# One rotation of six single PSUM banks in place of two mixing banks and two gram pairs

## The chip, the cores and the metric

The kernel runs on one core of a Trainium2 chip. The metric is device time in microseconds (us): the median of three runs. Beside it stands one profiled execution, whose trace gives start and length of each instruction; all times below that are not called a median are places or lengths in that execution, counted from the start of its span.

## The reference

An RWKV-6 attention block is followed by an MLP mixer. Batch 4, 8 heads, 768 steps, head width 48, all in fp32:

```python
for t in range(S):
    cur = einsum('bhd,bhe->bhde', u * k_t, v_t)
    y[:, :, t] = einsum('bhd,bhde->bhe', r_t, state + cur)
    state = w_t[..., None] * state + einsum('bhd,bhe->bhde', k_t, v_t)
x = y.transpose(0, 2, 1, 3).reshape(B, S, H * D)           # 4 x 768 x 384
h = relu(x^T @ w_tok1) @ w_tok2                             # over the 768 tokens, 256 hidden
u = x + h^T
out = u + relu(u @ w_ch1) @ w_ch2                           # over the 384 channels, 1536 hidden
```

## The kernel before

**Attention** is computed in chunks of 64 steps. A unit is 256 steps of one batch with all heads, so there are three units a batch and twelve in all. For each unit VectorE scans the decays twice (`ends` L354 and `begins` L362, over 112 x 1041 elements) and scales keys (L359) and queries (L365) by them. TensorE turns the keys (`tokens`, L276, copied out by ScalarE at L277), multiplies keys and queries of each chunk (`gram`, L248), makes the outer products of keys and values (`carry`, `kv_ps` L293), and then the outputs: the part from earlier chunks (`before`, `y_ps` L306) and that from within the chunk (`after`, L320). The gram is masked by VectorE into `at` (`mask`, L403). For the first four units there is a second gram with the bonus u (`own_gram`), put on the diagonal by a predicated copy (`own_put`, L376); later units get the diagonal from VectorE sums instead (L391). The states are passed from chunk to chunk by ScalarE (`scaled`, L416) and VectorE (`update`, L426, which reads `kv_ps`).

**Mixing** of a batch has these steps: `hidden` (L494) and `back` (L501, added to x by VectorE at L503) over tokens; `turn`, which transposes x (L510, copied out by ScalarE at L511); then for each 256 tokens `up` (twelve tiles `z_ps`, L518, taken by ScalarE with a relu at L520) and `down`. The first `down` is plain (L589, `h_ps`); all others are `quarters`: seven products `q_ps` of six matmuls each (L607) in Strassen's manner, from sums that VectorE makes of z (L648 to L650). The products are taken one by one: the first by ScalarE (L616), the next by VectorE at L621, L625, L629, L633, L639 and L645. The last batch uses `thirds` (L550) in place of `up`.

**Order.** The mixing of batch n is woven with the attention of batch n+1: `woven` merges the two lists by their shares of cost, and `strict` fixes the resulting order on TensorE, VectorE and ScalarE. So each of these engines runs a fixed list, in order. The attention of the first batch stands alone in front, with an order written out by hand; the last batch's mixing stands alone at the end.

**PSUM** has eight banks of 128 x 2 KiB. Until the last batch they belong to three pools: `ps_m`, two single banks that serve all mixing tiles (`h_ps`, `z_ps`, `q_ps`) and, in the first batch, the turned keys; `ps_g`, two pairs of banks for grams, turned keys and the transposes of x; and `ps_a`, one pair for `kv_ps` and `y_ps`. A tile may be written as soon as the readers of the tile that had its bank before are done. For the last batch, `ps_g` and `ps_a` are closed and six single banks (`ps_c`) take their place for `thirds` and the transposes, beside the two of `ps_m`.

A branch for rare inputs at the end (`by_halves`) is built from the same functions and is not executed here.

Of the kernel before, what the change touches and what calls it, by code (L numbers as in the profile page):

```python
# [10 lines left out]
f32 = mybir.dt.float32  # L11
# [9 lines left out]
DM = H * D  # L21
T = 64
C = S // 128
UC = 2
UB = C // UC
NU = B * UB
A = H // 2
# [3 lines left out]
X = UC * A  # L31
# [31 lines left out]
def rwkv6_then_mixer(  # L63
# [18 lines left out]
    pe, dve, act, pool, sp = nc.tensor, nc.vector, nc.scalar, nc.gpsimd, nc.sync  # L82
# [20 lines left out]
    xpool = ctx.enter_context(tc.tile_pool(name="xpool", bufs=2))  # L103
    wide = ctx.enter_context(tc.tile_pool(name="wide", bufs=1))
    mpool = ctx.enter_context(tc.tile_pool(name="mpool", bufs=2))
    ps_m = ctx.enter_context(tc.tile_pool(name="ps_m", bufs=2, space=bass.MemoryType.PSUM))
    six_banks = ctx.enter_context(ExitStack())

    def for_attention():
        return [six_banks.enter_context(tc.tile_pool(name=name, bufs=n, space=bass.MemoryType.PSUM)) for name, n in (("ps_g", 2), ("ps_a", 1))]  # L110

    ps_g, ps_a = for_attention()

    rks = [const.tile([128, 2 * COLS], f32, name=f"rk{i}") for i in range(3)]
    ws = [const.tile([128, WCOLS], f32, name=f"w{i}") for i in range(2)]
# [10 lines left out]
    strictly = const.tile([128, T], f32, name="strictly")  # L126
    diagonal = const.tile([128, T], u8, name="diagonal")
# [115 lines left out]

    def grams(k_, r_):

        g = ps_g.tile([128, 2, 512], f32, name="gram")
        for ca in range(X):
            fours(lambda q, j, rows, cols: pe.matmul(  # L248
                g[cols, q, ts(ca, T)], k_[rows, ds(ca * 128 + j * T, T)], r_[rows, ds(ca * 128 + j * T, T)],
                start=True, stop=True))  # L250
        return g.rearrange("p q (x t) -> p q x t", x=X)

    def over_heads(mask):
        return mask.unsqueeze(1).unsqueeze(1).to_broadcast([128, 2, X, T])

    def by_u(k_, uk, a):
        of, to = (t.rearrange("p (c a n) -> p c a n", c=UC, a=A)[:ROWS, :, a, :] for t in (k_, uk))
# [2 lines left out]
    def all_by_u(k_):  # L260
        uk = apool.tile([128, COLS], f32, name="near", bufs=1)
        for a in range(A):
            by_u(k_, uk, a)
        return uk

    def turned_keys(k_, apart=False):

        kT = apool.tile([128, UC, A, 128], f32, name="kT", bufs=1)
        if apart:
            both = [ps_m.tile([128, 512], f32, name="k_ps", tag="m").rearrange("p (a t) -> p a t", a=A) for c in range(UC)]  # L270
        else:
            both = ps_g.tile([128, 2, 512], f32, name="gram").rearrange("p c (a t) -> p c a t", a=A)
            both = [both[:, c] for c in range(UC)]
        for c in range(UC):
            for a in range(A):
                pe.transpose(both[c][:, a, :], k_[:, ts(c * A + a, 128)], ident)  # L276
        return kT, [lambda c=c: act.copy(kT[:, c], both[c]) for c in range(UC)]  # L277
# [50 lines left out]
    def unit(i):  # L328

        bt, half = divmod(i, UB)  # L330
        r_, k_ = (rks[i % 3][:, ts(n, COLS)] for n in range(2))
        w_, at = ws[i % 2], ats[i % 2]
        by_chunk = [t[:ROWS].rearrange("p (g t) -> p g t", t=T) for t in (r_, k_)]
        L = {"before": {}}
# [38 lines left out]
            L["own"] = grams(L.pop("uk"), r_)  # L373

        def own_put():
            dve.copy_predicated(out=at, mask=over_heads(diagonal), data=L.pop("own"))  # L376

        def products(n):
            t = nears[i]
# [11 lines left out]
            dve.copy_predicated(out=at, mask=over_heads(diagonal), data=of.unsqueeze(3).to_broadcast([128, 2, X, T]))  # L391

        def tokens():
            L["kT"], L["copies"] = turned_keys(k_, apart=bt == 0)

        def copied(c):
            L["copies"][c]()
# [2 lines left out]
            L["gram"] = grams(k_, r_)  # L400

        def mask():
            dve.tensor_mul(at, L.pop("gram"), over_heads(strictly))  # L403

        def carry():
            L["kv"] = outer(L.pop("kT"), vs[i], half, (ps_g, "gram") if i == UB - 1 else (ps_a, "a"))
# [78 lines left out]
    def mixing(bt, x_of, out_rows):  # L485
        last = bt == B - 1
# [17 lines left out]

        def turn(c):

            ps = bank("xT_ps") if last else ps_g.tile([128, 2, 512], f32, name="xT_ps", tag="gram")[:, 0]
            ps = ps[:, :DM].rearrange("p (m t) -> p m t", t=128)
            for m in range(DM // 128):
                pe.transpose(ps[:, m, :], x_of()[:, c, ts(m, 128)], ident)  # L510
            act.copy(xT[:, :, ts(c, 128)], ps)  # L511
# [155 lines left out]
    def steps(i):  # L667
# [38 lines left out]
           *e2["taken"], lambda: (load_w(3), load_rk(3), load_v(UB), load_w(4), load_rk(4)), to_ch[0][0], to_ch[1][0],  # L706
           *e1["ranges"], *h[8:], *e2["ranges"], lambda: sp.dma_start(u_rows, u_all))

    def single(steps, n):
        return [(0.1, f) for f in steps[n < 2:]]  # L710

# [2 lines left out]
    def verdict():  # L714
# [4 lines left out]
        dve.tensor_reduce(out=of_all[0:1], in_=total, axis=mybir.AxisListType.X, op=ALU.add)  # L719
        dve.tensor_scalar(beyond[0:1], of_all[0:1], 0.0, 1.0, op0=ALU.is_le, op1=ALU.is_lt)  # L720
        flagged.append(beyond)

    def bank(name):
        return ps_c.tile([128, 512], f32, name=name, tag="c")

    def last_mixing():
        hiddens, turned, rights, thirds, quarters = mixing_of(B - 1)
# [16 lines left out]
    for bt in range(B):  # L744
        ahead = []
        if bt == 0:
            to_ch = [single(e, n) for n, e in enumerate(to_ch)]
            both = [f for e in zip(ups[0], ups[1]) for f in e]
            ahead = woven(turned, sum(to_ch[:2], []))
            of_weights = [(0.1, lambda n=n: weight_sums(n)) for n in range(4)]  # L750
            pieces = woven(both, sum(to_ch[2:8], [])) + woven(downs[0][:6], to_ch[8]) + woven(downs[0][6:], of_weights[:3])
            pieces += downs[1][:4] + of_weights[3:] + downs[1][4:] + ups[2] + downs[2]
        elif bt < B - 1:
            hiddens, turned, ups, downs = mixing_of(bt)
            pieces = [e for h in hiddens for e in h] + turned
            *pieces, last = pieces
            ups[0].insert(2, last)
            for s in range(S // SEG):
                pieces += ups[s] + downs[s]
        else:  # L760
            six_banks.close()
            ps_c = six_banks.enter_context(tc.tile_pool(name="ps_c", bufs=6, space=bass.MemoryType.PSUM))
            pieces = last_mixing()
        n = (bt + 1) * UB
        att = [e for i in range(n, n + UB) if i < NU for e in steps(i)]
        strict(*(f for _, f in ahead + (woven(att, pieces) if att else pieces)))

    rare = nc.values_load(flagged[0][0:1, 0:1], min_val=0, max_val=1, skip_runtime_bounds_check_because="a comparison's result")

    six_banks.close()  # L770
    ps_g, ps_a = for_attention()

    def by_halves(b):

# [17 lines left out]
        for half in range(UB):  # L792
            r_, k_ = (rks[0][:, ts(n, COLS)] for n in range(2))
            w_, at = ws[0], ats[0]
            sp.dma_start(r_, rk[ds(b * UB + half, 1), 0].rearrange("o p n -> p (o n)"))
            sp.dma_start(k_, rk[ds(b * UB + half, 1), 1].rearrange("o p n -> p (o n)"))
            sp.dma_start(w_, w[ds(b * UB + half, 1)].rearrange("o p n -> p (o n)"))
            vt = vpool.tile([128, UC, DM], f32, name="vt")
            for c in range(UC):
                sp.dma_start(vt[:, c], v[ds(b, 1), ts(half * UC + c, 128), :].rearrange("o p e -> p (o e)"))  # L800
            dve.memset(at, 0.0)
            dve.copy_predicated(out=at, mask=over_heads(diagonal), data=grams(all_by_u(k_), r_))
            decay = rks[1][:, :COLS]
            act.copy(decay[:ROWS].rearrange("p (g t) -> p g t", t=T),
                     w_[:ROWS, :G * SEG1].rearrange("p (g s) -> p g s", s=SEG1)[:, :, 1:])
            for l in range(LEVELS):
                n = 1 << l
                dve.copy_predicated(out=at, mask=over_heads(level_masks[l]), data=grams(k_, r_))
                pair = decay[:ROWS].rearrange("p (m two) -> p m two", two=2)
                rr, kk = (t[:ROWS].rearrange("p (m two n) -> p m two n", two=2, n=n) for t in (r_, k_))  # L810
                for t, mine, other in ((rr, 1, 0), (kk, 0, 1)):
                    dve.tensor_mul(t[:, :, mine], t[:, :, mine], pair[:, :, other].unsqueeze(2).to_broadcast([ROWS, COLS // (2 * n), n]))
                longer = rks[1 + (l + 1) % 2][:, :COLS >> (l + 1)]
                dve.tensor_mul(longer[:ROWS], pair[:, :, 0], pair[:, :, 1])
                decay = longer
            by = decay[:ROWS].rearrange("p (x j) -> p x j", j=2)
            kv = outer(all_turned(k_), vt, half)
            for c in range(UC):
                for j in range(2):
                    g = 2 * (half * UC + c) + j  # L820
                    if g < 2 * C - 1:
                        new = states[g + 1] = apool.tile([128, A, D], f32, name="before", bufs=5)
                        got = kv[:ROWS, j, ds(c * A * D, A * D)].rearrange("p (a e) -> p a e", a=A)
                        if g == 0:
                            dve.tensor_copy(new[:ROWS], got)
                        else:
                            dve.tensor_mul(new[:ROWS], states[g][:ROWS], by[:, ts(c, A), j].unsqueeze(2).to_broadcast([ROWS, A, D]))
                            dve.tensor_add(new[:ROWS], new[:ROWS], got)
            y = across(r_, states, half)
            within(y, at, vt)  # L830
            for f in put_in(x, y, half):
                f()
# [42 lines left out]
```

## Time and profile before

| what | us |
|---|---|
| median of the runs (548.43 to 549.2) | 548.63 |
| the profiled execution | 550.15 |
| its span | 548.4 |
| TensorE busy (matmuls) | 507.8 |
| VectorE busy | 335.8 |
| ScalarE busy | 212.7 |

In the profile PE is TensorE's matmul side and PEld its weight loads, DVE is VectorE, ACT is ScalarE, SP is SyncE, which issues nearly all transfers. `L607` is line 607 of the kernel before. A row of the timeline gives the start, the length, the engine, line and operation, what it writes and reads, how many instructions it merges, and, in brackets, the idle time before it with what ended it. A matrix multiplication of fp32 stands as two instructions, so a product of six is x12. `x12` rows may be short of a record or two. In the list of waits, the numbers are the total, how often, and the longest. The first 60 us are mostly loads and the first batch's attention; after that, busy time of TensorE is given for stretches in the prediction.

### The profile page before, as it was taken

What the parts mean: (1) busy time and instruction counts of PE and PEld (TensorE: products, weight loads), DVE (VectorE), ACT (ScalarE), POOL (GpSimd) and SP (SyncE); (2) the same over time, 40 slices, a digit from 0 to 9 for tenths busy, and PEclk for the clock granted to TensorE, in tenths of its full rate; (3) what the DMA queues carried; (4) which work ended last, traced back from release to release, by engine and by line L of the source; (5) the groups of instructions that cost most, each with busy time, mean ns of one, the idle gap of its engine ahead of it and who ended that gap; (6) DMA issues with size and microseconds to landing.
All of it is one profiled execution on the core that took longest, in us unless ns stands there. A gap on an engine that the chain in (4) does not pass through costs nothing.

```text
span 548.4 us, 12596 instructions
## 1 busy us (share of the span) xinstructions
PE 507.8 (93%) x5542; PEld 435.3 (79%) x5542; DVE 335.8 (61%) x504; ACT 212.7 (39%) x525; POOL 1.3 (0%) x10
## 2 busy tenths in 40 slices
PE   3569899899799999999899999999999999999995
PEld 3556578666698868888888967888888968999995
DVE  7997599878772754192380665295393525775653
ACT  3676776662233333423323324413414313431300
POOL 0000000000000000000000000000000000000000
PEclk9678999899999999999999999999999999999999
DMA  8956656622231403203123113002000000000000
GB/s 304 330 165 209 182 178 241 172 89 84 87 108 34 139 17 117 59 32 125 46 78 92 45 44 99 30 1 88 1 30 1 2 29 2 1 1 31 0 31 33
DMA packets 20941, 46.01 MB, mean 84 GB/s; under 512 B 2128, under 2 KB 13008, under 8 KB 20880
## 3 DMA queue, kind: packets, MB, share of 16 engines
q1 hardware_dynamic: 20736, 45.14, 25.4%
q8 instruction: 45, 0.74, 0.6%
q14 instruction: 16, 0.13, 0.1%
q10 hardware_dynamic: 144, 0.00, 0.0%
HBM read 40.41 MB, written 4.72 MB: 82 GB/s over the span
## 4 chain that ended last, share of the span: by engine, by line
PE 72%; DVE 17%; ACT 6%; DMA 3%; issue 2%; SPq 0%; DVEq 0%; ACTq 0%
PE q_ps L607 21%; PE z_ps L518 21%; PE z_ps L550 6%; PE h_ps L494 5%; PE h_ps L501 4%; PE h_ps L589 3%; PE y_ps L306 3%; DVE to_end L354 3%; PE y_ps L320 2%; PE gram L248 2%; DMA rk<-in_rk_dram 2%; PE kv_ps L293 2%; PE gram L276 1%; DVE z L649 1%; ACT before L416 1%
## 5 line engine op out<-in xcount | busy, mean ns | idle before, releaser
L518 PE MATMUL z_ps<-xT,wch 128*128 128x256 f32 x648 | 149.1, 385 | 1.1 <-DVE o L645 1.1
L518 PEld LDWEIGHTS z_ps<-xT,wch 128*128 128x128 f32 x648 | 120.8, 191 | 18.9 <-DVE o L645 1.9
L607 PE MATMUL q_ps<-wch,z 128*128 128x192 f32 x492 | 87.4, 329 | 0.7 <-DVE o L629 0.5
L607 PEld LDWEIGHTS q_ps<-wch,z 128*128 128x128 f32 x492 | 80.3, 190 | 2.6 <-DVE o L629 1.1
L520 ACT ACTIVATE z<-z_ps 128x256 f32<-128x256 f32 x108 | 41.3, 382 | 84.8 <-PE z_ps L518 84.2
L607 PE MATMUL q_ps<-scratch,z 128*128 128x192 f32 x324 | 57.1, 328 | 3.5 <-DVE o L625 2.9
L607 PEld LDWEIGHTS q_ps<-scratch,z 128*128 128x128 f32 x324 | 52.9, 190 | 4.8 <-DVE o L625 3.8
L416 ACT ACTIVATE before<-state,to_end 112x48 f32<-112x48 f32 x176 | 44.2, 324 | 30.6 <-DVE state L426 28.0
L426 DVE TENSOR_TENSOR state<-before,kv_ps 112x192 f32<-112x192 f32 x40 | 14.0, 350 | 45.1 <-ACT before L416 29.0
L494 PE MATMUL h_ps<-x,wtok 128*128 128x384 f32 x96 | 33.9, 506 | 2.4 <-ACT x L326 2.0
L501 PE MATMUL h_ps<-h,wtok 128*128 128x384 f32 x96 | 35.4, 493 | 0.1
L503 DVE TENSOR_TENSOR x<-x,h_ps 128x384 f32<-128x384 f32 x24 | 13.3, 553 | 33.6 <-PE h_ps L501 33.4
L617 DVE TENSOR_TENSOR o<-x,z 128x192 f32<-128x192 f32 x8 | 2.9, 358 | 49.8 <-ACT z L616 46.7
L494 PEld LDWEIGHTS h_ps<-x,wtok 128*128 128x128 f32 x96 | 18.3, 195 | 14.6 <-ACT x L326 2.8
L354 DVE TENSOR_TENSOR_SCAN to_end<-w,starts 112x1041 f32<-112x1041 f32 (+1 forms) x13 | 28.1, 2160 | 2.0 <-DMA w<-in_w_dram 1.6
L362 DVE TENSOR_TENSOR_SCAN w<-w,starts 112x1041 f32<-112x1041 f32 x12 | 27.9, 2321 | 0.1
L346 ACT ACTIVATE junk<-to_end,least 112x1041 uint8<-112x1041 f32 x12 | 13.9, 1162 | 28.3 <-DVE to_end L354 28.3
L501 PEld LDWEIGHTS h_ps<-h,wtok 128*128 128x128 f32 x96 | 16.6, 190 | 9.6 <-ACT h L496 2.5
L326 ACT COPY x<-y_ps 64x384 f32<-64x384 f32 (+1 forms) x36 | 17.1, 475 | 18.3 <-PE y_ps L320 18.0
L306 PEld LDWEIGHTS y_ps<-before,rk 48*64 48x64 f32 x704 | 14.0, 144 | 12.3 <-issue 10.2
L306 PE MATMUL y_ps<-before,rk 48*64 48x48 f32 x704 | 15.4, 230 | 8.0 <-DVE state L426 8.0
L511 ACT COPY xT<-xT_ps 128x384 f32<-128x384 f32 x24 | 11.4, 476 | 22.0 <-PE xT_ps L510 22.0
(139 smaller groups left out, 668.3 us busy)
## 6 DMA issues: line engine op xcount, KB each, us to landing
rk<-in_rk_dram SPq DMA_DIRECT2D x36, 192.0 KB, 3.7
near<-in_near_dram SPq DMA_DIRECT2D x8, 768.0 KB, 4.5
w<-in_w_dram SPq DMA_DIRECT2D x11, 520.5 KB, 3.4
spare<-in_w_ch_dram SPq DMA_DIRECT2D x10, 512.0 KB, 4.8
vt<-in_v_dram SPq DMA_DIRECT2D x12, 384.0 KB, 3.8
out_dram<-o SPq DMA_DIRECT2D x24, 192.0 KB, 1.9
scratch<-in_w_ch_dram SPq DMA_DIRECT2D x8, 512.0 KB, 4.4
rk<-in_rk_dram SPq DMA_DIRECT2D x6, 512.0 KB, 8.4
```

Of the source, the lines that this page charges most:

```text
L306: pe.matmul(y[put(q, j), q, ds((c * A + a) * D, D)], r_[q * P:q * P + D, ds((c * A + a) * 128 + j * T, T)], before[g][q * P:q * P + D, a, ...
L326: return [lambda: act.copy(x[:, 0], got[:, 0])] + [lambda n=n: act.copy(x[ts(n, P), 1], got[ts(1 - n, P), 1]) for n in range(2)]
L354: dve.tensor_tensor_scan(to, of, start, 0.0, op0=ALU.mult, op1=ALU.add)
L362: dve.tensor_tensor_scan(w_[:ROWS], w_[:ROWS], starts[:ROWS], 0.0, op0=ALU.mult, op1=ALU.add)
L416: act.mul(t[:ROWS, a], state[bt, g][:ROWS, a], by_last(c, j)[:, a:a + 1])
L494: pe.matmul(sums[i], wtok1[:, c, ts(i, 128)], x_of()[:, c, :], start=(c == 0), stop=(c == C - 1))
L501: pe.matmul(ps, wtok2[:, i, ts(c, 128)], h1[:, i, :], start=(i == 0), stop=(i == DTOK // 128 - 1))
L518: pe.matmul(ps, wch1[:, m, ts(jt, 128)], xT[:, m, ts(s, SEG)], start=(m == 0), stop=(m == DM // 128 - 1))
L520: act.activation(zs[s][:, jt, :], ps, AF.Relu)
L550: pe.matmul(ps[:, q], lefts[r][:, ts(q, 128)], of[r], start=first and q == 0, stop=end and q == JB - 1, skip_group_check=True)
L589: pe.matmul(ps, zs[0][:, jt, ts(n, 128)], wch2[:, jt, :], start=(jt == 0), stop=(jt == NJ - 1))
L607: pe.matmul(ps, a[:, j, :], b[:, j, :], start=(j == 0), stop=(j == HJ - 1))
```

## The change

After the first batch's hand-ordered attention (which includes its token-mixing `hidden` step), `ps_g` and `ps_m` are closed, and one pool `ps_m` of six single banks takes their place until the end; `ps_a` keeps its pair throughout. So:

- mixing tiles (`h_ps`, `z_ps`, `q_ps`, and the last batch's `thirds`), grams, turned keys and the transposes of x all come from the six;
- a gram takes two single tiles instead of one pair. Its mask (L403 before) and the diagonal copy (L376 before) then become two instructions of 128 x 512 each instead of one of 128 x 1024;
- the turned keys always use two single tiles;
- in the last batch there are six banks for what had eight.

The function `bank` moves to the top, and nothing else of the order of work is touched. Lines move by up to three: L607 becomes L609, L518 becomes L520, L403 becomes L406, L426 becomes L429.

```diff
-    ps_m = ctx.enter_context(tc.tile_pool(name="ps_m", bufs=2, space=bass.MemoryType.PSUM))
+    ps_a = ctx.enter_context(tc.tile_pool(name="ps_a", bufs=1, space=bass.MemoryType.PSUM))
     six_banks = ctx.enter_context(ExitStack())
-
-    def for_attention():
-        return [six_banks.enter_context(tc.tile_pool(name=name, bufs=n, space=bass.MemoryType.PSUM)) for name, n in (("ps_g", 2), ("ps_a", 1))]
-
-    ps_g, ps_a = for_attention()
+    ps_g, ps_m = (six_banks.enter_context(tc.tile_pool(name=name, bufs=2, space=bass.MemoryType.PSUM)) for name in ("ps_g", "ps_m"))
+
+    def bank(name):
+        return ps_m.tile([128, 512], f32, name=name, tag="m")
...
     def grams(k_, r_):
 
-        g = ps_g.tile([128, 2, 512], f32, name="gram")
+        both = ps_g and ps_g.tile([128, 2, 512], f32, name="gram")
+        g = [both[:, q] for q in range(2)] if ps_g else [bank("gram") for q in range(2)]
         for ca in range(X):
             fours(lambda q, j, rows, cols: pe.matmul(
-                g[cols, q, ts(ca, T)], k_[rows, ds(ca * 128 + j * T, T)], r_[rows, ds(ca * 128 + j * T, T)],
+                g[q][cols, ts(ca, T)], k_[rows, ds(ca * 128 + j * T, T)], r_[rows, ds(ca * 128 + j * T, T)],
                 start=True, stop=True))
-        return g.rearrange("p q (x t) -> p q x t", x=X)
+        if ps_g:
+            return [(slice(0, 2), both.rearrange("p q (x t) -> p q x t", x=X))]
+        return [(slice(q, q + 1), g[q].rearrange("p (q x t) -> p q x t", q=1, x=X)) for q in range(2)]
+
+    def pick(at, mask, of):
+        for q, g in of:
+            dve.copy_predicated(out=at[:, q], mask=over_heads(mask, g.shape[1]), data=g)
...
-    def turned_keys(k_, apart=False):
+    def turned_keys(k_):
...
+        both = [bank("k_ps").rearrange("p (a t) -> p a t", a=A) for c in range(UC)]
...
         def mask():
-            dve.tensor_mul(at, L.pop("gram"), over_heads(strictly))
+            for q, g in L.pop("gram"):
+                dve.tensor_mul(at[:, q], g, over_heads(strictly, g.shape[1]))
...
-            ps = bank("xT_ps") if last else ps_g.tile([128, 2, 512], f32, name="xT_ps", tag="gram")[:, 0]
-            ps = ps[:, :DM].rearrange("p (m t) -> p m t", t=128)
+            ps = bank("xT_ps")[:, :DM].rearrange("p (m t) -> p m t", t=128)
...
+    six_banks.close()
+    ps_g, ps_m = None, six_banks.enter_context(tc.tile_pool(name="ps_m", bufs=6, space=bass.MemoryType.PSUM))
+
...
         else:
-            six_banks.close()
-            ps_c = six_banks.enter_context(tc.tile_pool(name="ps_c", bufs=6, space=bass.MemoryType.PSUM))
             pieces = last_mixing()
```

More of the change, by code (lines that the diff above doesn't have):

```diff
@@ L244, in grams, with over_heads @@
     def grams(k_, r_):
-        g = ps_g.tile([128, 2, 512], f32, name="gram")
+        both = ps_g and ps_g.tile([128, 2, 512], f32, name="gram")
+        g = [both[:, q] for q in range(2)] if ps_g else [bank("gram") for q in range(2)]
         for ca in range(X):
             fours(lambda q, j, rows, cols: pe.matmul(
-                g[cols, q, ts(ca, T)], k_[rows, ds(ca * 128 + j * T, T)], r_[rows, ds(ca * 128 + j * T, T)],
+                g[q][cols, ts(ca, T)], k_[rows, ds(ca * 128 + j * T, T)], r_[rows, ds(ca * 128 + j * T, T)],
                 start=True, stop=True))
-        return g.rearrange("p q (x t) -> p q x t", x=X)
-    def over_heads(mask):
-        return mask.unsqueeze(1).unsqueeze(1).to_broadcast([128, 2, X, T])
+        if ps_g:
+            return [(slice(0, 2), both.rearrange("p q (x t) -> p q x t", x=X))]
+        return [(slice(q, q + 1), g[q].rearrange("p (q x t) -> p q x t", q=1, x=X)) for q in range(2)]
+    def over_heads(mask, n=2):
+        return mask.unsqueeze(1).unsqueeze(1).to_broadcast([128, n, X, T])
+    def pick(at, mask, of):
+        for q, g in of:
+            dve.copy_predicated(out=at[:, q], mask=over_heads(mask, g.shape[1]), data=g)
     def by_u(k_, uk, a):
@@ L264, in all_by_u @@
         return uk
-    def turned_keys(k_, apart=False):
+    def turned_keys(k_):
         kT = apool.tile([128, UC, A, 128], f32, name="kT", bufs=1)
[L269 to L273, printed above, removed]
+        both = [bank("k_ps").rearrange("p (a t) -> p a t", a=A) for c in range(UC)]
         for c in range(UC):
@@ L375, in own_put @@
         def own_put():
-            dve.copy_predicated(out=at, mask=over_heads(diagonal), data=L.pop("own"))
+            pick(at, diagonal, L.pop("own"))
         def products(n):
@@ L393, in tokens @@
         def tokens():
-            L["kT"], L["copies"] = turned_keys(k_, apart=bt == 0)
+            L["kT"], L["copies"] = turned_keys(k_)
         def copied(c):
@@ L721, in verdict @@
         flagged.append(beyond)
-    def bank(name):
-        return ps_c.tile([128, 512], f32, name=name, tag="c")
     def last_mixing():
@@ L768, in rwkv6_then_mixer @@
     rare = nc.values_load(flagged[0][0:1, 0:1], min_val=0, max_val=1, skip_runtime_bounds_check_because="a comparison's result")
-    six_banks.close()
-    ps_g, ps_a = for_attention()
     def by_halves(b):
@@ L801, in by_halves @@
             dve.memset(at, 0.0)
-            dve.copy_predicated(out=at, mask=over_heads(diagonal), data=grams(all_by_u(k_), r_))
+            pick(at, diagonal, grams(all_by_u(k_), r_))
             decay = rks[1][:, :COLS]
@@ L807, in by_halves @@
                 n = 1 << l
-                dve.copy_predicated(out=at, mask=over_heads(level_masks[l]), data=grams(k_, r_))
+                pick(at, level_masks[l], grams(k_, r_))
                 pair = decay[:ROWS].rearrange("p (m two) -> p m two", two=2)
```

## The prediction

> **What bounds the kernel now.** I read the page first, then busy time by stage, then TensorE's waits from 60 us on, then the timeline around each wait. In the page, the total and the slices:
>
> ```profile
> PE 507.8 (93%) x5542; PEld 435.3 (79%) x5542; DVE 335.8 (61%) x504; ACT 212.7 (39%) x525; POOL 1.3 (0%) x10
> ...
> PE   3569899899799999999899999999999999999995
> ...
> PEclk9678999899999999999999999999999999999999
> ```
>
> TensorE is the bound engine from about 60 us on, and the digits are too coarse for what is left. Busy time by stage (window, its length, then PE):
>
> ```profile
> 110.00:150.00 40.00, 36.22 (x418) 27.21 (x414) 31.31 (x41) 14.49 (x34) 0.00 (x0) 1.00 0.28 85
> 150.00:232.00 82.00, 82.00 (x848) 68.86 (x840) 38.79 (x53) 30.66 (x85) 0.00 (x0) 1.00 0.26 81
> 232.00:316.00 84.00, 81.43 (x888) 74.05 (x888) 45.44 (x66) 27.47 (x79) 0.00 (x0) 1.00 0.22 68
> 316.00:358.00 42.00, 42.00 (x405) 31.91 (x404) 19.29 (x27) 16.14 (x43) 0.00 (x0) 1.00 0.18 56
> 358.00:442.00 84.00, 81.58 (x889) 74.24 (x888) 50.78 (x75) 27.00 (x78) 0.00 (x0) 1.00 0.06 20
> ```
>
> Two stages are solid. 232 to 316 and 358 to 442 have 2.57 and 2.42 us of holes, 110 to 150 has 3.78. The waits, TensorE alone, 60 to 548 us (total, times, longest):
>
> ```profile
> PE y_ps L306 <- DVE state L426: 4.6, 3, 2.4
> PE q_ps L607 <- DVE o L625: 2.9, 3, 1.6
> ...
> PE z_ps L518 <- DVE o L645: 1.1, 2, 0.6
> PE h_ps L589 <- ACT z L520: 0.7, 1, 0.7
> ...
> PE q_ps L607 <- DVE o L629: 0.5, 2, 0.2
> ```
>
> `q_ps` waiting for L625, L629, L633 and `z_ps` waiting for L645 are no data waits: those instructions read older, finished products out of PSUM. With two `ps_m` banks a product cannot start until the one two before it is taken. One such place, TensorE and then VectorE:
>
> ```profile
> 361.00 2.11 PE L607 MATMUL q_ps<-scratch,z 128*128 128x192 f32 x12
> 364.17 2.22 PE L607 MATMUL q_ps<-scratch,z 128*128 128x192 f32 x12 [1.05 <-DVE o L625]
> 366.63 2.22 PE L607 MATMUL q_ps<-wch,z 128*128 128x192 f32 x12 [0.24 <-DVE o L629]
> 368.69 1.04 PE L276 MATMUL gram<-ident,rk 128*128 128x128 f32 x8
> ```
> ```profile
> 361.29 2.33 DVE L354 TENSOR_TENSOR_SCAN to_end<-w,starts 112x1041 f32<-112x1041 f32 x1
> ...
> 363.82 0.30 DVE L625 TENSOR_TENSOR o<-o,q_ps 128x192 f32<-128x192 f32 x1
> 364.03 0.95 DVE L649 TENSOR_TENSOR z<-z 128x768 f32<-128x768 f32 x1
> 364.89 1.22 DVE L359 TENSOR_TENSOR rk<-rk,to_end 112x1024 f32<-112x1024 f32 x1
> ```
>
> The scan sits ahead of L625, whose input was complete at 361.2. Unhindered products start 1.95 us apart (230.37, 232.32, 234.27). A stop costs 0.1 us more than its idle time: the next group lasts 2.22 instead of 2.11.
>
> [...]those stops are the only ones in the two stages besides `y_ps`. [...]3.41 us at half clock from 106.7, after an idle of 2.38.
>
> **The change part by part.** The order of TensorE, ScalarE and SyncE instructions is the same in the built programs. VectorE gets ten instructions more. Starts below are those of the timeline, and "due" is the previous due start plus 1.95 (product) or 1.30 (`z_ps` group).
>
> C, 232 to 242: the fifth and sixth products start at 236.69 and 239.15; due 236.22 and 238.17. Their inputs are ready (L649 wrote the sums by 233.7 and 237.5). The key transposes behind start at 241.21, due 240.12, and their keys are ready at 238.64. Gain 1.09.
> D, 280: `z_ps` starts at 281.99, due 281.30; transposes 284.68, due 283.89. Gain 0.79.
> E, shown above: due 362.95, then 364.90, but L649 writes that input until 364.98, so 365.05 instead of 366.63. Gain 1.58. Keys, ready at 366.1, are in time for 367.1.
> F, 402 to 411: the last product 404.38, due 404.02 (input ready 403.46); `z_ps` 408.53, due 407.3; transposes 411.22, due 409.86, keys ready 409.6. Gain 1.36.
> Sum C to F: 4.82. What moves forward keeps its gain only if nothing later stops TensorE. The next `y_ps` (L306) waits for L426 to empty `ps_a`; at 309.6, 347.5, 391.7 and 434.2 that had happened 2.1 to 2.9 us before, more than any one gain. In E and F VectorE itself does not come forward, so it falls up to 1.6 behind TensorE, and this margin is what hides that; without it the gain would come back as a longer `y_ps` wait. At 267.79 it does stop (1.58), but VectorE's run before it starts at 264.69 with the copy of the block's first product, so it comes forward with TensorE.
>
> A, 105 to 150: `h_ps` L589 at 115.28 waits 0.69 for a bank; without it 0.85 earlier, until the `wch` conversion (L219, done 127.04) that its later part needs: 0.45 is left. It reaches `y_ps` at 147.52 through the store of `o` and VectorE's unbroken run from 139.03. The product waits at 140.84 and 144.64 (0.53 and 1.58) go too, but that run still ends at 147.3, so they only collect into one idle of some 2.6 us before `y_ps`. Bounds: 0.85 gained; 1.6 to 3.2 lost if that idle halves the clock. Near zero, taken as zero.
>
> Splits: a 128x1024 mask takes 1.13 us to the next start (140.71), a 128x512 one 0.60 (464.02), so two cost 0.07 more; ten times, 0.7 of VectorE. Hidden by VectorE's idle (at 255.72 it waits 0.78 for the gram anyway) except at 100, 102 and 141, where 0.2 in all sits ahead of `y_ps`; inside A's bounds. A new wait on TensorE can need an extra semaphore instruction: 23 more, 51 ns each in the trace, at most 1.2 us. Taken as nothing, since those before (181.6) leave the spacing at 1.95.
>
> New waits: transposes, grams and mixing now share banks, and TensorE runs in order, so behind one blocked tile everything would wait. I laid the changed program's bank addresses over the old times. No tile would start before its bank's last reader ended. The tightest are `z_ps` at 101.37 (0.34 after the mask, and the 2.38 stop follows anyway) and `xT_ps` at 204.86 and 329.96 (2.2 and 2.6). The last batch drops from eight banks to six; smallest margin 3.1. `kT` copies and `xT` stay as they are.
>
> The profiled execution is 550.15 with a span of 548.4; less 4.8, 545.3. The median of the runs is 1.5 below that execution, so from it 548.63 - 4.82 = 543.8.
>
> **Rivals.**
> Clock: the collected idle at 147 meets the window, 0.20. In favour: 2.38 did it at 105. Against: 1.58 did not at 144 and 267[...]. Price as at 105, where six `z_ps` took 2.58 for 1.46 and L320 1.72 for 1.15: 1.7, or twice that; 545.5 to 547.
> VectorE is the real bound: it has no idle from 357.65 to 375, so TensorE runs ahead and stops at a later VectorE result; only C and D remain, 546.7. Against: the margins of 2.1 to 2.9. 0.07.
> The rotation doesn't rotate, within 0.2%: banks are freed so that the pairs above still collide, or A's loss eats all. 0.06.
> Slower: strict turns. If a bank were taken oldest first whether free or not, the batch's own gram (83.2, taken only at 103.7) would hold two of six, and the fifth tile after it (90.91) would wait 12.8; less the 2.4 stop at 105 and the gain, 554. It decides as soon as four tiles follow a held gram. Against: the addresses give 90.91 another bank. 0.09, with a smaller such wait in it.
>
> **How the numbers follow.** Main case 0.58, 543.8, own range 542.9 (A at its best) to 544.8 (E or F a third smaller). 8 in 10 reach to the clock and VectorE cases: 542.7 to 546.7. About 0.2%, 1.1 us, can be told from no change. Faster 0.58 + 0.20 + 0.07 = 0.85; same 0.06; slower 0.09.
>
> **What would show it.** Right: waits of `q_ps` for L625 and L629 and of `z_ps` for L645 gone from the list, the two stages down to 81.5 or so, `y_ps` waiting before 147 longer than now. Wrong: `z_ps`, `k_ps` or `xT_ps` waiting for a mask or a copy; `PEclk` below 1.00 in 110 to 150; `y_ps` waits grown at 309, 391 or 434.

## The result

The changed kernel takes 544.55 us (median of 8 runs, 543.37 to 548.44) against 548.58 for the kernel before beside it (548.06 to 549.2): a ratio of 0.9935, interval 0.991 to 0.9961. Ten more runs in a second set, described below, gave 545.84 (543.72 to 549.05; ratio 0.9948, 0.9922 to 0.9975). So it is faster by 3 to 4 us. Its executions also lie further apart: over the 18 runs their standard deviation is 1.9, against 1.0 over the 82 runs of the kernel before that stand beside the experiments.

The profiled execution of the changed kernel took 544.09, its span is 542.3. First the page, with its totals, TensorE's slices and its clock:

```profile
PE 505.3 (93%) x5542; PEld 436.7 (81%) x5542; DVE 335.9 (62%) x514; ACT 212.4 (39%) x525; POOL 1.3 (0%) x10
...
PE   3578899899799999999899999999999999999995
...
PEclk9669999999999999999999999999999999999998
```

The work is the same, apart from ten more instructions on VectorE. The slices are again too coarse. Here are the same stretches as before (window, its length, then PE, PEld, DVE, ACT and POOL busy, then the granted clock):

```profile
110.00:150.00 40.00, 36.88 (x392) 28.57 (x392) 30.26 (x40) 15.78 (x37) 0.00 (x0) 0.96 0.29 88
...
232.00:316.00 84.00, 82.50 (x892) 75.10 (x891) 47.62 (x70) 27.20 (x78) 0.00 (x0) 1.00 0.24 75
...
358.00:442.00 84.00, 83.72 (x891) 75.22 (x890) 49.91 (x75) 27.35 (x79) 0.00 (x0) 1.00 0.07 25
```

The holes of the two solid stages went from 2.57 to 1.50 and from 2.42 to 0.28; what is left are waits of `y_ps`. In 110 to 150 the clock is at 0.96, where it was 1.00 before. TensorE's waits from 60 us on (total, times, longest):

```profile
PE y_ps L308 <- DVE state L429: 6.5, 3, 2.6
PE xT_ps L512 <- DVE x L506: 1.1, 1, 1.1
PE y_ps L322 <- ACT seen L314: 0.6, 2, 0.3
PE z_ps L552 <- ACT z L557: 0.2, 1, 0.2
PE h_ps L591 <- DVE wch L218: 0.2, 1, 0.2
PE q_ps L609 <- DVE z L651: 0.2, 1, 0.2
```

In this list no tile waits for a bank any more, except `y_ps`, which has its own pair as before: the waits of `q_ps` for L621, L625, L629 and L633, of `z_ps` for L645 and of `h_ps` for L520 are gone. The last two rows are waits for data. One new stop stands just ahead of the list's start, where the pools change:

```profile
59.32 2.85 PE L504 MATMUL h_ps<-h,wtok 128*128 128x384 f32 x8 [0.58 <-ACT h L499]
```

The first tile of the new pool starts only when ScalarE has taken both tiles that stood in the old banks. The eight traces in which the pools change here have this stop, the six in which they don't have none. It costs 0.47, but the wait for x at 68.04 before is then gone, and by the last transpose of x (71.31 before, 70.19 now) 0.10 is left of it.

The place that the prediction showed (before: products at 361.00, 364.17, 366.63) now reads, TensorE and then VectorE:

```profile
358.30 4.06 PE L609 MATMUL q_ps<-scratch,z 128*128 128x192 f32 x24
362.33 2.22 PE L609 MATMUL q_ps<-wch,z 128*128 128x192 f32 x12
364.38 1.04 PE L278 MATMUL k_ps<-ident,rk 128*128 128x128 f32 x8
```
```profile
358.59 2.33 DVE L356 TENSOR_TENSOR_SCAN to_end<-w,starts 112x1041 f32<-112x1041 f32 x1
...
361.12 0.29 DVE L627 TENSOR_TENSOR o<-o,q_ps 128x192 f32<-128x192 f32 x1
361.33 0.94 DVE L651 TENSOR_TENSOR z<-z 128x768 f32<-128x768 f32 x1
```

VectorE still comes late with L627, which takes a product out of PSUM behind the scan. TensorE no longer cares: two products follow each other without a break, and the third starts as L651 ends.

**The account.** Start of the same instruction in both executions, and the shift (after minus before):

| place | before | after | shift | step |
|---|---|---|---|---|
| `z_ps` behind the first woven `y_ps` | 110.43 | 109.30 | -1.13 | ahead of A |
| `y_ps` of the next unit | 147.52 | 145.22 | -2.30 | A: 1.17 sooner |
| `z_ps` two products later | 154.07 | 153.34 | -0.73 | A: 1.57 lost |
| last products of C | 239.15 | 237.44 | -1.71 | C: 0.98 |
| `y_ps` behind them | 267.79 | 265.88 | -1.90 | 0.19 |
| `z_ps` after D | 285.55 | 282.85 | -2.70 | D: 0.80 |
| product in E | 366.63 | 362.33 | -4.30 | E: 1.60 |
| `z_ps` after F | 412.10 | 406.43 | -5.67 | F: 1.37 |

From there to the last matmul nothing changes. C to F with the 0.19 give 4.94, and other traces repeat it: from the `y_ps` at 224.68 to that at 434.21 it takes 209.53 before, and 209.52 and 209.54 in two more kernels with the old banks (below, the splits alone and the warm kernel of before); it takes 204.59 in the changed kernel, and 204.58 to 204.64 in three more with five or six banks. The 1.13 in front is hardly the change's: it arose in the loads and the first batch's attention, and kernels with the old banks reach the same `z_ps` anywhere from 108.86 to 110.61. With the 0.39 behind the last matmul it makes these two executions differ by 6.06, where the medians differ by 4.0. How much of A's 1.17 is the change's is asked further down, under A.

**The loss in A.** The two stops for banks at 140.84 and 144.64 have indeed collected into one ahead of `y_ps`:

```profile
141.70 1.14 PE L609 MATMUL q_ps<-scratch,z 128*128 128x192 f32 x6
145.22 1.15 PE L308 MATMUL y_ps<-before,rk 48*64 48x48 f32 x64 [2.39 <-DVE state L429]
146.69 1.95 PE L322 MATMUL y_ps<-vt,at 64*64 64x48 f32 x64 [0.32 <-ACT seen L314]
148.57 4.93 PE L609 MATMUL q_ps<-wch,z 128*128 128x192 f32 x24
```

Windows over the stop and behind it:

```profile
142.00:145.00 3.00, 0.83 (x6) 0.54 (x4) 3.00 (x7) 2.16 (x6) 0.00 (x0) 1.00 0.00 0
...
147.00:150.00 3.00, 3.00 (x68) 2.91 (x61) 0.00 (x0) 1.28 (x3) 0.00 (x0) 0.50 0.58 143
```

After the stop the granted clock is 0.50 from 146.75 to 150.16. L322's 64 pairs last 1.95 instead of 1.15. From the start of `y_ps` to the start of `z_ps` it takes 8.12 instead of 6.55: 1.57 lost. This is the prediction's clock rival, a half clock behind the collected stop, with the sign that it named (`PEclk` below 1.00 in 110 to 150), and it came on top of the main case rather than in its place.

### The profile page after: what moved, and what is told of

The parts are those of the page before. It is cut to its first block, busy times and chain, and to the rows that moved or that the text cites. A ratio compares the mean times of both kernels' runs of the same rounds, so it can differ in the third digit from the quotient of the medians.

```text
span 542.3 us, 12629 instructions
## 1 busy us (share of the span) xinstructions
PE 505.3 (93%) x5542; PEld 436.7 (81%) x5542; DVE 335.9 (62%) x514; ACT 212.4 (39%) x525; POOL 1.3 (0%) x10
## 4 chain that ended last, share of the span: by engine, by line
PE 75%; DVE 15%; ACT 4%; DMA 3%; issue 2%; SPq 0%; DVEq 0%; ACTq 0%
PE q_ps L609 26%; PE z_ps L520 21%; PE z_ps L552 6%; PE h_ps L504 5%; PE h_ps L497 5%; PE y_ps L322 3%; PE y_ps L308 3%; DMA rk<-in_rk_dram 2%; PE gram L248 2%; DVE scratch L212 2%; PE kv_ps L295 1%; DVE wch L218 1%; PE k_ps L278 1%; DVE w L364 1%; PE xT_ps L512 1%
## 5 line engine op out<-in xcount | busy, mean ns | idle before, releaser
L520 PE MATMUL z_ps<-xT,wch 128*128 128x256 f32 x648 | 148.0, 384 | 0.0
L520 PEld LDWEIGHTS z_ps<-xT,wch 128*128 128x128 f32 x648 | 121.0, 190 | 16.6 <-DVE wch L218 0.3
L609 PE MATMUL q_ps<-wch,z 128*128 128x192 f32 x492 | 87.8, 330 | 0.0
L609 PEld LDWEIGHTS q_ps<-wch,z 128*128 128x128 f32 x492 | 81.1, 191 | 1.3 <-DVE z L651 0.3
L609 PE MATMUL q_ps<-scratch,z 128*128 128x192 f32 x324 | 56.5, 327 | 0.2 <-DVE z L651 0.2
L609 PEld LDWEIGHTS q_ps<-scratch,z 128*128 128x128 f32 x324 | 53.0, 190 | 0.6 <-issue 0.4
L429 DVE TENSOR_TENSOR state<-before,kv_ps 112x192 f32<-112x192 f32 x40 | 14.0, 350 | 40.1 <-ACT before L419 28.1
L497 PE MATMUL h_ps<-x,wtok 128*128 128x384 f32 x96 | 32.5, 490 | 2.8 <-ACT x L328 2.6
```

The source lines that it names most:

```text
L497: pe.matmul(sums[i], wtok1[:, c, ts(i, 128)], x_of()[:, c, :], start=(c == 0), stop=(c == C - 1))
L520: pe.matmul(ps, wch1[:, m, ts(jt, 128)], xT[:, m, ts(s, SEG)], start=(m == 0), stop=(m == DM // 128 - 1))
L609: pe.matmul(ps, a[:, j, :], b[:, j, :], start=(j == 0), stop=(j == HJ - 1))
```

## Experiments

Theory: the gain is C to F, worth 4.9, because a mixing product no longer waits for VectorE to empty the bank of the one two before it; A gives up to 1.2, which a half clock behind the collected stop takes back in some executions. Rivals: the gain comes from elsewhere (the splits, the stretch ahead of 105, A); the half clock has nothing to do with the stop; the depth of six is what counts.

### The rotation only from the second batch on

```diff
-    six_banks.close()
-    ps_g, ps_m = None, six_banks.enter_context(tc.tile_pool(name="ps_m", bufs=6, ...))
...
         strict(*(f for _, f in ahead + (woven(att, pieces) if att else pieces)))
+        if bt == 0:
+            six_banks.close()
+            ps_g, ps_m = None, six_banks.enter_context(tc.tile_pool(name="ps_m", bufs=6, ...))
```

Until then, turned keys and the transposes of x take `ps_g` and `ps_m` as before.

> The rotation of six begins only when the first batch's mixing is done (190 us), so A (105 to 150) keeps its two mixing banks and two gram pairs; C to F have the six. If the gain is C to F alone, as the prediction's sum says, time is before less 4.8 to 5.0: 543.7, no q_ps wait for L625 or L629 after 190, and the stops at 140.8, 144.6 and 147.5 stand as before (0.5, 1.6, 0.7), none long enough to halve the clock at 147, so its executions lie closer together than the changed kernel's (543.4 to 548.4). If A was worth its 1.2 us and the half clock there is rare, this is 1.2 slower than the changed kernel's best, 544.6. If the gain came from A or from the first 105 us, it is above 546.

Measured: 544.72 (5 runs, 544.5 to 545.04), ratio 0.9917, interval 0.9901 to 0.9933. Its waits:

```profile
PE y_ps L312 <- DVE state L433: 4.5, 3, 2.4
PE q_ps L614 <- DVE o L632: 1.6, 1, 1.6
...
PE h_ps L501 <- DVE starts L356: 0.4, 1, 0.4
```

The one `q_ps` wait is A's, at 142.88. C to F are free: against before, the trace moves forward by 0.98 in C, 0.99 in D with the stretch ahead of it, 1.60 in E and 1.37 in F, which is the same 4.94. A new wait of 0.45 stands where the pools change (188.10), and with what follows it costs 0.71 until the next `y_ps`. Even so it equals the changed kernel's median without A. So C to F alone carry the gain, and A with the rotation is worth about nothing on the median, as a gain and a risk that cancel. Its five executions lie within 0.54 of each other; that the short stops in A make them so is not shown, since the late rotation with four banks (below) keeps the same A and spreads over 4.3.

### The splits alone

```diff
-            dve.tensor_mul(at, L.pop("gram"), over_heads(strictly))
+            g = L.pop("gram")
+            for q in range(2) if i >= UB else [slice(0, 2)]:
+                q = slice(q, q + 1) if i >= UB else q
+                dve.tensor_mul(at[:, q], g[:, q], over_heads(strictly)[:, q])
```

In the kernel before, with its pools, for the units from the second batch on (`i >= UB`); the diagonal copy likewise.

> Before, with the ten masks and the diagonal copy each in two instructions of 128x512; banks as before. If the splits cost nothing (0.7 us of VectorE, hidden): 548.4 to 549.0, within 0.1% of before. If each 0.07 sits on the path: 549.3. If the extra instruction and its wait on TensorE cost more: 549.5 or above.

Measured: 548.94 (14 runs, 546.13 to 551.54), ratio 0.9999, interval 0.9983 to 1.0016. The ten added VectorE instructions cost nothing that can be measured, as put down in the prediction.

### How many banks

> As the late rotation, but with four single banks, two left unused. The bank addresses laid over the old times show no tile waiting in C to F, and three waits of 0.69 in the last batch's z_ps (467, 481, 509), where six tiles are wanted: 2.1 more than the late rotation, 545.8, with C to F as fast. If the gain needs the depth of six, q_ps or z_ps wait at 236 to 242, 363 to 367 or 404 to 411 and it is 547 or above. If the late stops are hidden: 543.7.

> The changed kernel with five banks in the rotation, one left unused. Laid over the changed kernel's trace, the only tiles without a free bank are the five z_ps from 93.5 to 98.7, which then follow each other in the one bank that the own gram (two) and the gram (two) leave: about 0.85 each, 4.0 in all; 2.6 of it goes into the stop before the y_ps at 104, 1.4 remains, and the half clock after that stop (1.2) may go: 543.3 to 546, no q_ps or z_ps wait for a bank anywhere after 105. If banks are taken in strict turns, such waits stand in C to F too, 550 or more.

The edits are `bufs=4` in the late rotation and `bufs=5` in the changed kernel. Four banks: 546.87 (9 runs, 544.68 to 549.0; ratio 0.9963, 0.9943 to 0.9983), 2.15 above the late rotation. C to F have no bank wait in the list, only one too short for it: the `z_ps` at 241.91 starts 2.17 behind the group before it instead of 1.95, and with its after-effects 0.33 is lost up to the next `y_ps`. The three waits are in the last batch, where they were expected:

```profile
463.80 1.16 PE L557 MATMUL z_ps<-xT,rk 128*128 128x128 f32 x8 [0.57 <-ACT z L562]
...
478.55 1.16 PE L557 MATMUL z_ps<-xT,rk 128*128 128x128 f32 x8 [0.57 <-ACT z L562]
```

Five banks: 544.48 (4 runs, 543.09 to 545.2; ratio 0.9923, 0.99 to 0.9945). Four bank waits are those of `z_ps` tiles that share one bank while the two grams hold four, and a fifth stands ahead of them, for ScalarE's copy of the turned keys:

```profile
84.59 3.72 PE L520 MATMUL z_ps<-xT,wch 128*128 128x256 f32 x16 [0.38 <-ACT kT L279]
...
95.35 1.56 PE L520 MATMUL z_ps<-xT,wch 128*128 128x256 f32 x6 [0.35 <-ACT z L522]
97.38 1.56 PE L520 MATMUL z_ps<-xT,wch 128*128 128x256 f32 x6 [0.47 <-ACT z L522]
99.42 1.56 PE L520 MATMUL z_ps<-xT,wch 128*128 128x256 f32 x6 [0.47 <-ACT z L522]
101.46 1.78 PE L520 MATMUL z_ps<-xT,wch 128*128 128x256 f32 x7 [0.47 <-ACT z L522]
```

Their sum lands in the stop ahead of the `y_ps` at 104, which was there anyway. Of the five tiles expected four waited. Each stood idle for 0.47, and the groups are 2.04 apart instead of 1.30: a stop costs 0.74 here, about a quarter of a microsecond beside its idle time, near the 0.85 expected. The wait at 84.59 had not been expected. Two things follow. For C to F four banks do what six do, but for the 0.33; three were not tried. And the way the prediction found new waits, by laying the changed program's bank addresses over the old times, names most of the tiles, not all: it missed this one, and the stop where the pools change.

### Is it the stop that halves the clock?

```diff
         def before():
...
+            if i in (UB, UB + 1):
+                idle = bank("idle")
+                for n in range(10):
+                    pe.matmul(idle[:, :128], ident, ident, start=True, stop=True)
             L["y"] = across(r_, L["before"], half)
```

> The changed kernel with ten more 128x128 matmuls of the identity (their product is used by nobody) on TensorE ahead of the y_ps at 104 and ahead of that at 145, where TensorE stood still for 2.60 and 2.39. [...] If the half clock follows the idle: PEclk 1.00 from 104 to 112 and from 145 to 152, 1.2 and 1.6 us less of execution where the changed kernel had them, no execution above 545, median 542 to 543. If the half clock comes from elsewhere: as the changed kernel, 544.6, with executions up to 548. If the ten are longer than the stops they push y_ps: 545 or more.

Measured: 541.65 (4 runs, 541.42 to 543.0), ratio 0.9867, interval 0.9847 to 0.9888. TensorE's timeline and a window of it:

```profile
141.88 2.39 PE L437 MATMUL idle<-ident 128*128 128x128 f32 x20
144.21 1.15 PE L308 MATMUL y_ps<-before,rk 48*64 48x48 f32 x64
145.69 1.15 PE L322 MATMUL y_ps<-vt,at 64*64 64x48 f32 x64 [0.33 <-ACT seen L314]
```
```profile
146.00:149.00 3.00, 3.00 (x73) 2.95 (x65) 0.00 (x0) 1.43 (x3) 0.00 (x0) 1.00 0.80 175
```

Ten useless matmuls at each of two stops make the kernel 2.9 faster than the changed kernel's first set, and 4.2 than its second. At 145 they take 2.33 from their start to that of `y_ps`, nearly as long as the stop of 2.39. Even so `y_ps` comes no later: 35.30 behind the `z_ps` that follows the first woven `y_ps`, against 35.92 in the changed kernel. L322 is back at 1.15, and the clock is at 1.00 from 60 to 530 (the mean over the whole span is 0.978, against 0.972 in the changed kernel). With the stop filled, the 0.50 that stood behind it is gone: in this pair of traces the stop is shown to be its cause.

The same edit in the kernel before, at its stop at 105 alone, was to isolate what the banks give when no half clock interferes:

> The kernel before with the ten spare matmuls ahead of its y_ps at 105 alone (its other stops are too short for them). If they only keep the clock there: 1.2 less where it was halved, about 547.7. The warm kernel (541.65) then differs from this one by what the six banks give when no half clock takes any of it back: 6.1 if A is worth its 1.2 as the traces say, 4.9 if A is worth nothing.

Measured: 549.54 (22 runs), ratio 1.0013, interval 0.9998 to 1.0028. The expectation fell, and the run doesn't answer its question. TensorE and then ScalarE:

```profile
104.38 2.50 PE L434 MATMUL idle<-ident 128*128 128x128 f32 x20 [2.07 <-ACT z L524]
```
```profile
103.96 0.36 ACT L524 ACTIVATE z<-z_ps 128x256 f32<-128x256 f32 x1
```

With two `ps_m` banks the spare tile itself waited 2.07 for a bank, until ScalarE took a `z_ps` at 103.96; so the matmuls ran behind the stop and pushed `y_ps` to 106.8. It is the shortage of two banks once more, and the edit had overlooked it.

### The changed kernel once more

> The changed kernel as it is, beside the others on one chip. If half clocks after its long stops (2.6 at 104, 2.4 at 145) come and go with the window's phase: executions from 543.3 to 548.5 in steps of about 1.5, median 544 to 546, and a share of full clock that is lower in the longer ones. If the early spread was one chip's: within 1 us of each other.

Measured: 545.84 (10 runs, 543.72 to 549.05). The spread of the first set came again. From each run's span and mean granted clock the number of half-clock windows can be worked out: 2 x (1 - clock) x span / 3.41. Over both sets (18 runs) it has a mean of 9.1, with 7.6 in the two fastest runs and 10.9 in the slowest of each set; a straight line through the 18 gives 1.5 us for each window, with a correlation of 0.90. So in the changed kernel the half clocks make most of the spread. The 82 runs of the kernel before beside the experiments have a mean of 7.4 windows and a mean time of 548.95. They too reach from 546.53 to 552.18, but there the windows explain less (0.7 us each, correlation 0.56). The changed kernel has 1.7 windows more, worth 2.5 by its own line. As an estimate, 4.94 for C to F and 0.4 to 1.2 for A, less 2.5, is 2.8 to 3.6, where the means (545.77 for the changed kernel) differ by 3.2.

This execution (547.88) shows it happening twice in a row, in windows laid on the grid of its half clocks:

```profile
142.43:145.84 3.41, 1.02 (x29) 0.76 (x32) 3.41 (x6) 2.04 (x6) 0.00 (x0) 1.00 0.00 0
145.84:149.25 3.41, 3.10 (x119) 2.94 (x109) 0.97 (x3) 0.16 (x1) 0.00 (x0) 0.50 0.21 70
149.25:152.67 3.42, 3.42 (x18) 3.33 (x13) 0.00 (x0) 1.43 (x3) 0.00 (x0) 0.50 0.59 170
```

TensorE stood still for 2.39 in the first; the next two ran at 0.50.

### What else keeps `y_ps` waiting

The three stops left (104, 145, 266) wait for the last state update, L429, and VectorE's list has a diagonal copy (L260 or L393, 1.3 us) ahead of it that only L322 needs. So it was moved:

```diff
-                (1.3, e["sums_put"] if by_tokens else e["own_put"]), (0.4, e["ranges"][1]), (0.7, up[3]),
+                (0.4, e["ranges"][1]), (0.7, up[3]), (1.3, e["sums_put"] if by_tokens else e["own_put"]),
```

> The changed kernel with the diagonal copy (L260 or L393, 1.3 us of VectorE) behind the last state update in every unit, instead of ahead of it. If the remaining y_ps stops are VectorE's list: those at 104, 145 and 266 fall by 1.2 to 1.3 each, 3.8 in all, and the half clock at 106 and 146 goes; 539.5 to 541.5. Against: VectorE then waits about 1.0 for ScalarE's scaling between the last two updates, where the copy filled that time; if that holds, y_ps moves by 0.3 to 0.5 each, 543 to 544.

> The kernel before with the diagonal copy behind the last state update, banks as before. The y_ps stops at 105, 147 and 268 fall by 1.2, 0.66 and 1.58, the half clock after 105 mostly goes (0.9): 544.5. If the banks' gain adds to it, the same move with six banks (538.6) is 5.9 to 6.2 faster than this. If the move also brings VectorE's reading of the products forward, the stops for two banks shrink by themselves: 542 to 543, and the banks are worth 4 or less beside it.

With six banks: 538.6 (5 runs, 538.2 to 540.84; ratio 0.9819, 0.9802 to 0.9835). With the banks of before: 544.67 (6 runs, 543.76 to 547.81; ratio 0.9923, 0.9893 to 0.9954). VectorE, in the changed kernel and then with the copy moved:

```profile
142.21 0.95 DVE L651 TENSOR_TENSOR z<-z 128x768 f32<-128x768 f32 x1
143.08 1.30 DVE L393 COPY_PREDICATED at<-diagonal,sums 128x1024 f32<-128x1024 uint8 x1
144.28 0.54 DVE L631 TENSOR_TENSOR o<-x,q_ps 128x384 f32<-128x384 f32 x1
144.73 0.34 DVE L429 TENSOR_TENSOR state<-before,kv_ps 112x192 f32<-112x192 f32 x1
```
```profile
143.04 0.95 DVE L651 TENSOR_TENSOR z<-z 128x768 f32<-128x768 f32 x1
143.93 0.35 DVE L429 TENSOR_TENSOR state<-before,kv_ps 112x192 f32<-112x192 f32 x1
144.20 0.55 DVE L631 TENSOR_TENSOR o<-x,q_ps 128x384 f32<-128x384 f32 x1
144.67 1.30 DVE L393 COPY_PREDICATED at<-diagonal,sums 128x1024 f32<-128x1024 uint8 x1
```

With six banks the stops fall from 2.60, 2.39 and 1.50 to 1.43, 0.78 and none; mostly it was the copy that set them, and not ScalarE's scaling. In neither trace does a half clock stand between 62 and the last matmul (the mean over the span is 0.978 in both). So these two come nearest to what the warm kernel of before was to give, the worth of the six banks where no half clock takes anything back. Their medians differ by 6.07. That is not a clean price: the runs (standard deviations 1.1 and 1.5) leave it uncertain by some 1.5 us, and the moved copy brings the old banks one more stop, 0.25 at 385.20, so that the traces differ by 5.38 over C to F (208.40 against 203.02) and not by 4.94. C to F at least are there in full; whether A adds its part is not settled.

The other candidate on VectorE's list is the fourth weight sum (L465, 1.35 us), moved from behind the fourth entry of `downs[1]` to behind the ninth:

```diff
-            pieces += downs[1][:4] + of_weights[3:] + downs[1][4:] + ups[2] + downs[2]
+            pieces += downs[1][:9] + of_weights[3:] + downs[1][9:] + ups[2] + downs[2]
```

> The changed kernel with one VectorE instruction moved: the fourth weight sum (L465, 1.35 us at 140.4) goes behind the last state update that the y_ps at 145 waits for. If VectorE's list sets that y_ps: y_ps at about 143.9, stop 1.1 instead of 2.39, half clock after 146 gone; 1.3 better than the changed kernel at its best, 542 to 543.3, with no execution above 545. If the seventh product then waits for the weight sum, the gain is given back: 544.5.

> Both of these. If the two add: stop at 145 gone (2.4), those at 104 and 266 down by 1.3, no half clock after 105: 538.5 to 540.5. If ScalarE's scaling sets the last update: 541.5 to 543.

Alone: 545.58 (22 runs, 541.59 to 548.91; ratio 0.9942, 0.9925 to 0.9959), so the expectation fell. The stop shrank only to 2.00, since the weaving put another sum of z (L652, 0.95) ahead of the update in the same move, and behind 2.00 the half clock still stood (mean clock 0.64 in 146 to 150). Both: 540.74 (4 runs, 539.9 to 541.3), by the medians 2.1 slower than the copy alone, though the ranges overlap. The stop at 145 is gone, but the seventh product then waits 1.31 for L465, which stands behind everything else on VectorE; those two idle stretches were still followed by a half clock at 145.6 (mean clock 0.62 in 146 to 150). With the sum behind the seventh entry, directly after the copy:

> Six banks, the diagonal copy behind the last update, and the weight sum L465 directly behind that copy rather than at the end of VectorE's list for this stage (where the seventh product waited 1.3 for it). y_ps at 144.4 loses its 0.78, the output part behind it part of its 0.54, and the seventh product finds its sum ready by 0.3: 0.8 to 1.1 better than the diagonal copy alone, 537.6. If the product waits for the sum: 538.6 or more.

Measured: 538.3 (6 runs, 536.7 to 539.18; ratio 0.9797, 0.9772 to 0.9822). In the trace `y_ps` starts without a wait at 142.67 and the product without one at 145.23, 0.64 in all by the shifts; the medians differ by 0.3 and their ranges overlap. These two beat both kernels; which of them is the better is not settled.

## Why the prediction was right

**Size.** It said 543.8 with a range of 542.7 to 546.7; 544.55 and 545.84 were measured. The mechanism and the sum hold. C: 0.98 for 1.09. D: 0.80 for 0.79. E: 1.60 for 1.58. F: 1.37 for 1.36. Together 4.75 for 4.82; with 0.19 at the stop at 267, which the sum had left out, 4.94.

**Margins.** The step that the gain would not come back as a longer `y_ps` wait at 309, 391 or 434 held: none of these stands in the list of waits. The rival in which VectorE is the real bound would have kept only C and D.

**Splits, semaphore instructions and new waits.** All put down at nothing. The splits alone measured 0.9999. No tile of the rotation waits for a bank in the changed kernel, except the first, at 59.32, where the pools change; the prediction had not seen that one, and 0.10 is left of it. The addresses also foretold most of the places where four and five banks would hurt. The rival of strict turns (own gram blocking the tile at 90.91) did not come about: no bank wait stands there.

**A.** This term was mis-sized, on both sides. It was taken as zero, with 0.85 at best; `y_ps` came 1.17 sooner. Of that, 0.65 is the bank wait of `h_ps` (0.85 less 0.20 given back in the wait for L218, where the prediction had left 0.45). The rest, some 0.5, is within what chance does here: VectorE's run towards `y_ps` begins when a store of `o` has landed, and that differs between executions with the same banks. VectorE before, and in the warm kernel of before:

```profile
139.03 0.36 DVE L617 TENSOR_TENSOR o<-x,z 128x192 f32<-128x192 f32 x1 [3.12 <-DMA out_dram<-o]
```
```profile
137.30 0.36 DVE L621 TENSOR_TENSOR o<-x,z 128x192 f32<-128x192 f32 x1 [1.38 <-DMA out_dram<-o]
```

From the `z_ps` behind the first woven `y_ps` to the next unit's `y_ps`, five traces that keep the old banks and VectorE's order in A (before, the splits alone, the warm kernel of before, and the late rotation with six and with four) take 35.35 to 37.09. Their mean is 36.23, and the kernel before's is the longest. Two of the changed kernel and one with five banks take 35.84 to 35.92. Against that mean the change gains about 0.4 in A, an estimate from these eight traces. The loss was named and priced right (1.6 to 3.2 in the bounds, 1.57 measured for one window), but its chance was not. The failing step is the one that gave the clock rival 0.20 and held against it that "1.58 did not at 144 and 267". A stop of 2.4 was not like one of 1.58, and even those of 1.5 at 266 were followed by a half clock in one of the two traces of the changed kernel and in the one with four banks (0.50 from 267.25 to 270.66). In four traces with a stop of 2.0 to 2.45 at 145 (the changed kernel twice, five banks, the sum moved), all four were followed by a half clock (0.50 from 146.75 and from 145.84 in the changed kernel; mean clock 0.64 in 146 to 150 in each of the others). By the count of windows above, this is why the median stands 0.75 to 2 above the forecast and not on it.

**Clock.** The length of 3.41 held: from 60 us to the end of the matmuls each half clock lasts 3.41 or twice that, on one grid in each execution (before: 106.67 to 110.08; changed: 105.79 to 109.20 and 146.75 to 150.16, whose starts lie 40.96 apart, twelve times that). After how long a standstill one follows, the trace before had not shown: 2.38 had one behind it, 1.58 had none. Every stop from 60 us on is shorter than 3.41 (the longest in the changed kernel is 2.60), and still a half clock follows some.

## What to carry over

Where a product is taken out of PSUM by an engine that also has long instructions in its list, count the banks from the longest such instruction: here a scan of 2.33 us against products 1.95 apart needed more than two and no more than four. Removing the stops for banks on an engine that then met a data wait collected them into one long stop (0.53, 1.58 and 0.66 became 2.39). On TensorE the long stop cost more here than the short ones had, because the clock behind it was 0.50 for 3.41 us; reordering the list that feeds the wait helped (538.6), and so did spare matmuls in the stop, with which the clock stayed at 1.00 (541.65). Lay the new bank addresses over the old trace before building on a rotation, and look for the tiles that hold their bank long and for the place where the pools change. And before a shift between two traces is put down to the change, see how much the same stretch differs among traces without it.

## What had not been expected of the hardware

A fixed grid of 3.41 us could be read off each trace from its half-clock windows, and TensorE's idle time counted in each step of it. Over the fourteen traces, from 60 us to 530, all eleven steps in which TensorE stood still for 1.67 us or more were followed by a half clock; of eleven with 1.43 to 1.64, four were; of those with less, only one, which was itself at half clock (145.84 in the execution shown above). In the kernel before, the step from 103.26 has 1.95 of idle time and the next runs at 0.50; those from 140.81 and 144.22, with 1.19 and 1.08 from the stops of 0.53, 1.58 and 0.66, have 1.00 behind them. In the changed kernel the steps from 102.38 and 143.34, with 1.72 and 2.20, have 0.50 behind them, and the one from 262.80, with 1.50, has 1.00. So in these traces 1.67, about half a step, was enough each time; what decided between 1.43 and 1.64 was not settled here. If 1.67 is taken as the limit, a stop of 2.4 is followed by a half clock in about (3.41 + 2.4 - 2 x 1.67) / 3.41 = 0.7 of the positions of the grid, an estimate from these numbers. The position differs from one execution to the next (a step begins at 143.34 in one trace of the changed kernel and at 142.43 in the other), and with it the number of half clocks. A kernel without long stops in A was not free of it: four banks with the late rotation, where A is as before, lie within 4.3 us of each other in nine executions, and the profiled one has the half clock from 267.25 behind the stop of 1.50 at 266. So the 0.54 of the late rotation with six, in five executions, may be luck.
